# Small operations moved between engines, weight conversions spread over a slot: attention and a bilinear FFN on one Trainium2 core

## The chip, the core and the metric

The kernel runs on one core of a Trainium2 chip. A core has TensorE (PE, matrix products into PSUM), VectorE (DVE), ScalarE (ACT), GpSimd (POOL, which works on SBUF only here) and DMA queues issued mostly by SyncE (SP). Each engine runs its own instructions in the order of the program and waits on semaphores for the others. The metric is device time of one execution in microseconds (us), the median of several runs.

## The reference

An attention block with a threshold feeds a bilinear FFN. Everything is float32 on input and output; the three FFN weights arrive as float64 and are turned into float32 on the chip.

```python
# q, k, v: (8 batches, 8 heads, 576 rows, 64)    tau: 0.02
scores = scale * np.matmul(q, k.transpose(0, 1, 3, 2))
thresh = np.max(scores, axis=-1, keepdims=True) - tau
scores = np.where(scores >= thresh, scores, -1000000000.0)
scores = scores - np.max(scores, axis=-1, keepdims=True)
attn = np.exp(scores)
attn = attn / (np.sum(attn, axis=-1, keepdims=True) + 1e-09)
x = np.matmul(attn, v)          # reshaped to (4608, 512)
# ... w_a, w_b: (512, 1536), w_out: (1536, 512)
out = ((x @ w_a) * (x @ w_b)) @ w_out
```

## The kernel before

The program is a list of 160 units of attention (a pair of heads, a block of rows), one in each slot g, with matmuls of the FFN handed out between them by `advance(cols)`, which issues FFN steps until so many columns are done. The first 16 slots also convert the weights: 36 pieces of 128 x 512 float64 numbers, two or three a slot. A piece takes two activations on ScalarE (upper half and lower half), a clamp on GpSimd, then, one slot later, a sign and a shift on VectorE and an integer add on GpSimd:

```python
    def convert_first(n):
        if n not in raws:
            return
        raw, top = raws[n], pieces[n][0]
        low = work.tile([P, CW], FP32, tag="osb", bufs=OSB_BUFS, name="low")
        nc.scalar.activation(top, raw[:, :, 1].bitcast(FP32), AF.Abs)
        nc.scalar.activation(low, raw[:, :, 0], AF.Copy, bias=2.0, scale=2.0 ** -51)
        stages[n] = low
    def convert_clamp(n):
        if n in stages:
            top = pieces[n][0]
            nc.gpsimd.tensor_scalar(top, top, float_of(0x47EFFFFF), float_of(0x38000000),
                                    op0=ALU.min, op1=ALU.max)
    def convert_sign(n):
        if n in stages:
            low, hi = stages[n].bitcast(U32), raws.pop(n)[:, :, 1]
            nc.vector.scalar_tensor_tensor(out=low, in0=hi, scalar=0x80000000, in1=low,
                                           op0=ALU.bitwise_and, op1=ALU.bitwise_or)
            if n in taken:
                extra.append(taken.pop(n))
    def convert_shift(n):
        if n in stages:
            top = pieces[n][0].bitcast(U32)
            nc.vector.tensor_scalar(top, top, 3, None, op0=ALU.logical_shift_left)
    def convert_add(n):
        if n in stages:
            top, low = pieces[n][0].bitcast(I32), stages.pop(n).bitcast(I32)
            nc.gpsimd.tensor_tensor(top, top, low, op=ALU.add)
            state["converted"] += 1
```

In a slot the scores are made by TensorE, the maxima of their rows by VectorE; a bias for the exponential and a threshold for the mask follow, on GpSimd until the sums of the output weights are made (`state["sums"]`, slot 20), afterwards on ScalarE and VectorE:

```python
        mx = small.tile([P, 2], FP32, tag="mx", name="mx")
        thr = small.tile([P, 2], FP32, tag="thr", name="thr")
        bias = small.tile([P, 2], FP32, tag="bias", name="bias")
        for j in range(n):
            c = slice(j, j + 1)
            nc.vector.tensor_reduce(mx[:, c], sc[j], axis=AX.XY, op=ALU.max)
            if not state["sums"]:
                nc.gpsimd.tensor_scalar(bias[:, c], mx[:, c], e_nscale, None, op0=ALU.mult)
        engine = nc.vector if state["sums"] else nc.gpsimd
        engine.tensor_scalar(thr[:, 0:n], mx[:, 0:n], cut, None, op0=ALU.subtract)
        scored[i, u] = (sc, thr, bias, mx, not state["sums"])

    def weigh(i, u):
        sc, thr, bias, mx, biased = scored.pop((i, u))
        n = len(sc)
        sums = small.tile([P, 2], FP32, tag="sums", name="sums")
        ws = rooms_of(i, u)
        sb = [s.rearrange("p c (n e) -> p c n e", e=Q) for s in sc]
        wb = [w.rearrange("p (c n) e -> p c n e", c=2) for w in ws]
        for j in range(n):
            if not biased:
                nc.scalar.activation(bias[:, j:j + 1], mx[:, j:j + 1], AF.Copy, scale=e_nscale)
            nc.scalar.activation(wb[j], sb[j], AF.Exp, bias=bias[:, j:j + 1], scale=e_scale)
        for j in range(n):
            wv = wb[j]
            nc.vector.scalar_tensor_tensor(
                out=wv, in0=sb[j], scalar=thr[:, j:j + 1], in1=wv,
                op0=ALU.is_ge, op1=ALU.mult, accum_out=sums[:, j:j + 1])
        weights[i, u] = (ws, sums)
```

`sc` holds two of the four PSUM tiles until the mask has read them. In the first eight slots (BY_PE = 8) the normalised weights are turned by TensorE with a diagonal matrix of reciprocals; after that ScalarE normalises and VectorE transposes blocks, with a swap through DRAM:

```python
    def reciprocal(i, u, engine):
        ws, sums = weights[i, u]
        n = len(ws)
        if engine is nc.scalar:
            nc.scalar.activation(sums[:, 0:n], sums[:, 0:n], AF.Copy, bias=1e-9)
        else:
            nc.vector.tensor_scalar_add(sums[:, 0:n], sums[:, 0:n], 1e-9)
        rcp = small.tile([P, 2], FP32, tag="rcp", name="rcp")
        nc.vector.reciprocal(rcp[:, 0:n], sums[:, 0:n])
        weights[i, u] = (ws, rcp)
# ...
    def diagonals(i, u):
        ws, rcp = weights[i, u]
        dg = work.tile([P, 2, P], FP32, tag="h", bufs=H_BUFS, name="dg")
        for j in range(2):
            nc.scalar.activation(dg[:, j], ident, AF.Copy, scale=rcp[:, j:j + 1])
        weights[i, u] = (ws, dg)

    def turn_pe(i, u):
        ws, dg = weights.pop((i, u))
        ws = [w.rearrange("p n e -> p (n e)") for w in ws]
        wT = work.tile([P, NSLOT, P], FP32, tag="wT", bufs=WT_BUFS, name="wT")
        turned[i, u, "pe"] = wT
        tp = banks(512, "tp").rearrange("p j (s q) -> p j s q", s=NT)
        for j, w in enumerate(ws):
            for s in range(NT):
                c = TAIL * j + s * P
                nc.tensor.matmul(tp[:, j, s, :], w[:, c:c + P], dg[:, j], start=True, stop=True)
        for j in range(2):
            nc.scalar.copy(wT[:, 5 * j:5 * j + NT], tp[:, j])
        tp = banks(P, "tp")[:, 0]
        for j, w in enumerate(ws):
            c = MAIN * (1 - j)
            nc.tensor.matmul(tp[TAIL * j:TAIL * (j + 1)], w[:, c:c + TAIL], dg[:, j],
                             start=True, stop=True)
        nc.vector.tensor_copy(wT[:, NT], tp)
# ...
def join(out, lo, hi):
    nc.scalar.copy(out, lo)
    nc.vector.tensor_tensor(out, out, hi, op=ALU.add)
```

`weighted_unit` and `weighted` multiply the turned weights with v into `pv`, join it into `xT`, and GpSimd copies `xT` with its halves of partitions swapped into `xS` (`exchange`). The FFN waits, while the program is being written, for the count of converted pieces; its first product goes through ScalarE, its second through VectorE:

```python
        for f, c0, c1 in steps:
            while (state["converted"] < 2 * HP * (f // n + 1)
                   or kind == "first" and state["rows"] * P < c1):
                yield 0, 0, 0
            # ... pab: 32 matmuls for w_a, then 32 for w_b, on xT and xS
                if w is wa_sb:
                    nc.scalar.copy(ht, pab)
                else:
                    nc.vector.tensor_tensor(ht, ht, pab, op=ALU.mult)
```

The loop over slots, with the parts that play a role here:

```python
    for g in range(len(units) + PV_LAG):
        written = len(pending)
        here = g < len(units)
        converting = bool(early.get(g)) or bool(early.get(g - 1))
        if here:
            i, u = units[g]
            scores(i, u)
        turn_back()
        exchange_blocks()
        pace = (PACE if g > BY_PE else PACE_EARLY) * BLOCK_COLS
        if g > BY_PE:
            pace = min(pace, backlog() / (min([a for a in arrivals if a > g] + [len(units) + PV_LAG + 1]) - g))
        pace += (NSLOT + 1) // 2 * S / (NT + 1) + CATCH_UP * max(backlog() - BLOCK_COLS, 0)
        if 2 <= g < BY_PE + 2:
            weighted_unit(*units[g - 2])
            running["owed"] -= (NSLOT + 1) // 2 * P
        if g < 3:
            prep_copy(*prep_pe(g + 1, "q"))
        for n in early.get(g - 1, []):
            convert_sign(n)
        for n in early.get(g - 1, []):
            convert_shift(n)
        for n in early.get(g - 1, [])[-1:] + early.get(g - 1, [])[:-1]:
            convert_add(n)
        if g == 3:
            for c in range(0, NSUM - 2 * CW + 1, 2 * CW):
                extra.append(sums_u32[:, c:c + 2 * CW].rearrange("p (f w) -> p f w", w=2))
        load_weights(RAWS)
        if g > BY_PE and g <= len(units):
            turn_blocks(*units[g - 1])
        if g > BY_PE:
            advance(PORTIONS[0] * pace)
        if here:
            weigh(i, u)
        if 0 < g <= BY_PE:
            turn_pe(*units[g - 1])
        if g < 3:
            prep_copy(*prep_pe(g + 1, "k"))
        for p in range(HP, NPR):
            for name, d in (("q", 2), ("k", 1)):
                if g == first[p] - d:
                    prep(p, name)
        if g > BY_PE:
            advance(PORTIONS[1] * pace)
            n = g - PV_LAG
            if BY_PE <= n < len(units) and part(*units[n]):
                make_room()
                weighted(*part(*units[n]))
                running["owed"] -= (NSLOT + 1) // 2 * width(*part(*units[n]))
        for n in early.get(g, [])[:1]:
            convert_first(n)
            convert_clamp(n)
        if here:
            reciprocal(i, u, nc.scalar if converting else nc.vector)
        if here and g < BY_PE:
            diagonals(i, u)
        elif here:
            normalise(i, u)
        for n in early.get(g, [])[1:]:
            convert_first(n)
            convert_clamp(n)
        load_weights(RAWS)
        for p in range(HP, NPR):
            for name, d in (("q", 4), ("k", 3)):
                if g == first[p] - d:
                    load(p, name)
        for p in range(1, NPR):
            if g == first[p] - 1:
                load_v(p)
        store(written)
        advance((PORTIONS[2] if g > BY_PE else sum(PORTIONS[:3])) * pace)
        advance(PORTIONS[3] * pace)
```

## Time and profile before

| | before |
|---|---|
| median of 3 runs | 1483.07 us (1481.49 to 1487.32) |
| profiled execution, span | 1478.9 us |
| TensorE busy | 1425.3 us, 25344 matmul instructions |
| VectorE, ScalarE, GpSimd busy | 925.8, 669.7, 360.1 us |
| first 160 us: TensorE, VectorE, ScalarE, GpSimd busy | 119.3, 109.6, 100.8, 101.0 us |
| granted clock of TensorE | 0.991 |

In a timeline each line gives the start, the duration, the engine, the line of the kernel (L367 is line 367), the operation, output and inputs by the program's names, the shapes and a count of instructions; in brackets stands how long the engine had been idle before it and what ended that. In this kernel L332 is the maximum, L334 and L363 the bias on GpSimd and on ScalarE, L336 the threshold, L364 the exponential, L367 the mask, L225 and L226 the conversion's activations, L238 and L246 sign and shift, L232 and L251 clamp and add, L584 and L586 the FFN's copy and product into h, L468 and L469 the two halves of a join, L489 the swapped copy, L325 scores, L479 pv, L406 and L412 the transposes and L408 their copies, L578 the FFN's first products.

### The profile page before, as it was taken

What the parts mean: (1) busy time and instruction counts of PE and PEld (TensorE: products, weight loads), DVE (VectorE), ACT (ScalarE), POOL (GpSimd) and SP (SyncE); (2) the same over time, 40 slices, a digit from 0 to 9 for tenths busy, and PEclk for the clock granted to TensorE, in tenths of its full rate; (3) what the DMA queues carried; (4) which work ended last, traced back from release to release, by engine and by line L of the source; (5) the groups of instructions that cost most, each with busy time, mean ns of one, the idle gap of its engine ahead of it and who ended that gap; (6) DMA issues with size and microseconds to landing.
All of it is one profiled execution on the core that took longest, in us unless ns stands there. A gap on an engine that the chain in (4) does not pass through costs nothing.

```text
span 1478.9 us, 57127 instructions
## 1 busy us (share of the span) xinstructions
PE 1425.3 (96%) x25344; PEld 1201.8 (81%) x25344; DVE 925.8 (63%) x2068; ACT 669.7 (45%) x1213; POOL 360.1 (24%) x563
## 2 busy tenths in 40 slices
PE   5777999999999999999999999999999999999998
PEld 4666587898879898898888788889888888888886
DVE  5767677778767776675645766577756766622212
ACT  4766355555544554553533544355444554411010
POOL 3876522204030312122222213130404040310000
PEclk9999999999999999999999999999999999999999
DMA  9957888789868976786547876588756976530000
GB/s 192 214 154 184 169 168 191 175 178 194 209 139 169 193 174 144 176 184 163 125 118 137 183 164 150 119 188 184 158 138 138 193 174 158 135 90 16 2 17 16
DMA packets 624582, 220.75 MB, mean 149 GB/s; under 512 B 542928, under 2 KB 612048, under 8 KB 624336
## 3 DMA queue, kind: packets, MB, share of 16 engines
q1 hardware_dynamic: 621968, 216.52, 66.8%
q8 instruction: 199, 3.26, 0.9%
q10 hardware_dynamic: 2368, 0.59, 0.2%
q14 instruction: 47, 0.39, 0.1%
HBM read 127.40 MB, written 89.65 MB: 147 GB/s over the span
## 4 chain that ended last, share of the span: by engine, by line
PE 86%; DVE 5%; DMA 3%; ACT 2%; SPq 2%; issue 1%; POOL 1%; ACTq 0%; DVEq 0%; POOLq 0%
PE pab L578 47%; PE po L621 19%; PE sc L325 10%; PE pv L479 10%; PE po L665 1%; DVE tw L433 1%; DVE low L238 1%; DVE mx L332 1%; DMA swap<-tw 1%; DVE tw L367 1%; DMA raw<-in_moe_w_b_dram 1%; SPq L206 1%; SPq L151 0%; SPq L441 0%; DMA sums_u<-in_k_dram 0%
## 5 line engine op out<-in xcount | busy, mean ns | idle before, releaser
L332 DVE TENSOR_REDUCE mx<-sc 128x1 f32<-128x576 f32 x288 | 205.1, 749 | 133.0 <-PE sc L325 122.2
L578 PE MATMUL pab<-xS,wa_sb 64*64 64x256 f32 (+1 forms) x3584 | 271.6, 371 | 0.9 <-POOL xS L489 0.9
L578 PE MATMUL pab<-xS,wb_sb 64*64 64x256 f32 (+1 forms) x3584 | 268.2, 372 | 0.0
L325 PE MATMUL sc<-kT,qT 64*64 64x288 f32 x2304 | 243.4, 413 | 19.2 <-DVE kT L312 8.1
L590 POOL TENSOR_TENSOR h<-h 128x256 f32<-128x256 f32 x168 | 117.4, 733 | 542.1 <-PE po L621 539.0
L578 PE MATMUL pab<-xT,wa_sb 64*64 64x256 f32 (+1 forms) x3200 | 237.6, 371 | 5.3 <-POOL thr L336 2.1
L578 PE MATMUL pab<-xT,wb_sb 64*64 64x256 f32 (+1 forms) x3200 | 235.2, 368 | 5.6 <-DVE h L586 4.1
L621 PE MATMUL po<-wo_sb,h 64*64 64x256 f32 x3264 | 240.1, 376 | 0.0
L386 ACT ACTIVATE tw<-tw,rcp 128x576 f32<-128x576 f32 x244 | 176.1, 768 | 130.1 <-DVE rcp L380 129.9
L364 ACT ACTIVATE tw<-sc,bias,scalars 128x576 f32<-128x576 f32 x260 | 214.7, 832 | 38.3 <-POOL bias L334 25.4
L578 PEld LDWEIGHTS pab<-xS,wa_sb 64*64 64x64 f32 x3584 | 192.4, 133 | 31.3 <-POOL xS L489 5.3
L367 DVE SCALAR_TENSOR_TENSOR tw<-sc,thr,tw 128x576 f32<-128x576 f32 x260 | 203.6, 802 | 20.7 <-ACT tw L364 19.8
L578 PEld LDWEIGHTS pab<-xS,wb_sb 64*64 64x64 f32 x3584 | 193.6, 134 | 25.2 <-issue 0.8
L621 PEld LDWEIGHTS po<-wo_sb,h 64*64 64x64 f32 x3264 | 176.0, 132 | 24.8
L578 PEld LDWEIGHTS pab<-xT,wa_sb 64*64 64x64 f32 x3200 | 170.4, 134 | 30.4 <-DVE kept L469 4.3
L578 PEld LDWEIGHTS pab<-xT,wb_sb 64*64 64x64 f32 x3200 | 169.6, 133 | 27.9 <-DVE h L586 4.5
L479 PE MATMUL pv<-wT,vm 64*64 64x320 f32 (+3 forms) x2592 | 187.2, 381 | 3.1 <-ACT h L584 1.6
L325 PEld LDWEIGHTS sc<-kT,qT 64*64 64x64 f32 x2304 | 143.3, 135 | 52.5 <-issue 14.4
L621 PE MATMUL po<-sums_u,h 64*64 64x256 f32 x2448 | 180.6, 376 | 0.0
L433 DVE STREAM_TRANSPOSE tw<-tw 128x576 f32<-128x576 f32 x240 | 171.6, 753 | 0.2 <-ACT tw L386 0.2
L586 DVE TENSOR_TENSOR h<-h,pab 128x512 f32<-128x512 f32 (+1 forms) x112 | 73.3, 655 | 147.9 <-PE pab L578 140.1
L479 PEld LDWEIGHTS pv<-wT,vm 64*64 64x64 f32 x2592 | 141.6, 135 | 26.3 <-issue 2.8
(85 smaller groups left out, 1236.9 us busy)
## 6 DMA issues: line engine op xcount, KB each, us to landing
swap<-tw SPq DMA_DIRECT2D x240, 288.0 KB, 5.2
wT<-swap SPq DMA_DIRECT2D x28, 1440.0 KB, 7.8
wT<-swap SPq DMA_DIRECT2D x32, 1152.0 KB, 6.3
vm<-in_v_dram SPq DMA_DIRECT2D x32, 288.0 KB, 4.8
qT<-in_q_dram SPq DMA_DIRECT2D x112, 72.0 KB, 3.6
kT<-in_k_dram SPq DMA_DIRECT2D x112, 72.0 KB, 5.1
swap<-wt SPq DMA_DIRECT2D x112, 72.0 KB, 2.7
out_dram<-kept SPq DMA_DIRECT2D x30, 256.0 KB, 4.5
```

Of the source, the lines that this page charges most:

```text
L206: engine.dma_start(dst, part)
L325: nc.tensor.matmul(sc[j if u < NT else 0][to, c], qT[r, q0:q0 + D], kT[r, c * SH:(c + 1) * SH], start=True, stop=True)
L332: nc.vector.tensor_reduce(mx[:, c], sc[j], axis=AX.XY, op=ALU.max)
L364: nc.scalar.activation(wb[j], sb[j], AF.Exp, bias=bias[:, j:j + 1], scale=e_scale)
L367: nc.vector.scalar_tensor_tensor(out=wv, in0=sb[j], scalar=thr[:, j:j + 1], in1=wv, op0=ALU.is_ge, op1=ALU.mult, accum_out=sums[:, j:j + 1])
L386: nc.scalar.activation(w, w, AF.Copy, scale=rcp[:, j:j + 1])
L433: nc.vector.transpose(w, w)
L479: nc.tensor.matmul(pv[j * D:(j + 1) * D, r], vm[rows, k0], wT[rows, k0], start=(s == (NT if j == r else 0)), stop=(s == NT - 1))
L578: nc.tensor.matmul(pab[c * D:(c + 1) * D, r], w[rows, f // n, k, fs + c * D:fs + (c + 1) * D], moving, start=(k == 0), stop=(k == H - 1))
L586: nc.vector.tensor_tensor(ht, ht, pab, op=ALU.mult)
L590: (nc.vector if state["over"] else nc.gpsimd).tensor_tensor(*a, **kw)
L621: nc.tensor.matmul(po[c * D:(c + 1) * D, r, y], ht[rows, t0:t0 + D], other[rows, f], start=(f == 0), stop=(f == NF // 2 - 1))
```

## The change

Five things are changed. The bias is made by ScalarE and the threshold by VectorE in every slot, so GpSimd has no part in the softmax. The three steps that end a piece's conversion (sign, shift, add) are no longer done for all pieces at the start of a slot: the first piece's are done there, the second's after the masks and the normalisation, the third's after the FFN's share. In slots 0 to 8 that share of the FFN is issued ahead of the conversions' first steps of the second and third piece. In slots 0 to 7 the reciprocal is taken right after the masks, its sum on VectorE. And since pieces are now finished in the middle of a slot, the count that the FFN looks at is brought up to date only at the start of the next slot. The aim is that masks and h copies need not stand behind conversions in their engines' queues.

```diff
--- before.py
+++ after.py
@@ -182,7 +182,7 @@
         pieces.append((wo_sb[:, F, :], [w_out[F * P:(F + 1) * P, :].bitcast(U32)]))
     NPIECES = len(pieces)
     raws, stages, extra, taken = {}, {}, [], {}
-    state = {"loaded": 0, "converted": 0, "rows": 0, "sums": False, "through": 0, "over": False}
+    state = {"loaded": 0, "added": 0, "converted": 0, "rows": 0, "sums": False, "through": 0, "over": False}
 
 
     NSUM = NF // 2 * 3 * CH
@@ -249,7 +249,7 @@
         if n in stages:
             top, low = pieces[n][0].bitcast(I32), stages.pop(n).bitcast(I32)
             nc.gpsimd.tensor_tensor(top, top, low, op=ALU.add)
-            state["converted"] += 1
+            state["added"] += 1
 
 
     scalars = const.tile([P, 8], FP32, name="scalars")
@@ -330,11 +330,8 @@
         for j in range(n):
             c = slice(j, j + 1)
             nc.vector.tensor_reduce(mx[:, c], sc[j], axis=AX.XY, op=ALU.max)
-            if not state["sums"]:
-                nc.gpsimd.tensor_scalar(bias[:, c], mx[:, c], e_nscale, None, op0=ALU.mult)
-        engine = nc.vector if state["sums"] else nc.gpsimd
-        engine.tensor_scalar(thr[:, 0:n], mx[:, 0:n], cut, None, op0=ALU.subtract)
-        scored[i, u] = (sc, thr, bias, mx, not state["sums"])
+        nc.vector.tensor_scalar(thr[:, 0:n], mx[:, 0:n], cut, None, op0=ALU.subtract)
+        scored[i, u] = (sc, thr, bias, mx)
 
     def rooms_of(i, u):
 
@@ -352,15 +349,14 @@
 
     def weigh(i, u):
 
-        sc, thr, bias, mx, biased = scored.pop((i, u))
+        sc, thr, bias, mx = scored.pop((i, u))
         n = len(sc)
         sums = small.tile([P, 2], FP32, tag="sums", name="sums")
         ws = rooms_of(i, u)
         sb = [s.rearrange("p c (n e) -> p c n e", e=Q) for s in sc]
         wb = [w.rearrange("p (c n) e -> p c n e", c=2) for w in ws]
         for j in range(n):
-            if not biased:
-                nc.scalar.activation(bias[:, j:j + 1], mx[:, j:j + 1], AF.Copy, scale=e_nscale)
+            nc.scalar.activation(bias[:, j:j + 1], mx[:, j:j + 1], AF.Copy, scale=e_nscale)
             nc.scalar.activation(wb[j], sb[j], AF.Exp, bias=bias[:, j:j + 1], scale=e_scale)
         for j in range(n):
             wv = wb[j]
@@ -748,6 +744,14 @@
     for name in ("q", "k"):
         prep_copy(*prep_pe(0, name))
     early = {}
+
+    def convert_rest(g, k):
+
+        for n in early.get(g - 1, [])[k:k + 1]:
+            convert_sign(n)
+            convert_shift(n)
+            convert_add(n)
+
     n = 0
     for g in range(NPIECES):
         size = min(3 if 4 <= g < 10 else 2, NPIECES - n)
@@ -755,6 +759,7 @@
         n += size
     for g in range(len(units) + PV_LAG):
         written = len(pending)
+        state["converted"] = state["added"]
         here = g < len(units)
         converting = bool(early.get(g)) or bool(early.get(g - 1))
         if here:
@@ -771,12 +776,7 @@
             running["owed"] -= (NSLOT + 1) // 2 * P
         if g < 3:
             prep_copy(*prep_pe(g + 1, "q"))
-        for n in early.get(g - 1, []):
-            convert_sign(n)
-        for n in early.get(g - 1, []):
-            convert_shift(n)
-        for n in early.get(g - 1, [])[-1:] + early.get(g - 1, [])[:-1]:
-            convert_add(n)
+        convert_rest(g, 0)
         if g == 3:
             for c in range(0, NSUM - 2 * CW + 1, 2 * CW):
                 extra.append(sums_u32[:, c:c + 2 * CW].rearrange("p (f w) -> p f w", w=2))
@@ -787,6 +787,8 @@
             advance(PORTIONS[0] * pace)
         if here:
             weigh(i, u)
+        if here and g < BY_PE:
+            reciprocal(i, u, nc.vector)
         if 0 < g <= BY_PE:
             turn_pe(*units[g - 1])
         if g < 3:
@@ -805,12 +807,15 @@
         for n in early.get(g, [])[:1]:
             convert_first(n)
             convert_clamp(n)
-        if here:
-            reciprocal(i, u, nc.scalar if converting else nc.vector)
         if here and g < BY_PE:
             diagonals(i, u)
         elif here:
+            reciprocal(i, u, nc.scalar if converting else nc.vector)
             normalise(i, u)
+        convert_rest(g, 1)
+        if g <= BY_PE:
+            advance(pace)
+        convert_rest(g, 2)
         for n in early.get(g, [])[1:]:
             convert_first(n)
             convert_clamp(n)
@@ -823,8 +828,9 @@
             if g == first[p] - 1:
                 load_v(p)
         store(written)
-        advance((PORTIONS[2] if g > BY_PE else sum(PORTIONS[:3])) * pace)
-        advance(PORTIONS[3] * pace)
+        if g > BY_PE:
+            advance(PORTIONS[2] * pace)
+            advance(PORTIONS[3] * pace)
 
         if not converting and not state["sums"]:
             state["slots"] = state.get("slots", 0) + 1
```

## The prediction, made before the changed kernel had run

> **What bounds the kernel now.** I read the page's busy line and its 40 slices first, to see where TensorE has gaps at all.
>
> ```profile
> PE 1425.3 (96%) x25344; PEld 1201.8 (81%) x25344; DVE 925.8 (63%) x2068; ACT 669.7 (45%) x1213; POOL 360.1 (24%) x563
> ...
> PE   5777999999999999999999999999999999999998
> ```
>
> TensorE is busy 1425.3 of 1478.9 us, so only 53.6 us of gaps exist, and the row of digits puts them at the start. Busy time by stretch says it in numbers (columns: stretch, its length, then busy us and instructions of PE, PEld, DVE, ACT, POOL, then granted clock, DMA share, GB/s):
>
> ```profile
> 0.00:160.00 160.00, 119.32 (x2150) 98.17 (x2154) 109.56 (x242) 100.79 (x189) 101.00 (x144) 0.93 0.81 185
> 160.00:230.00 70.00, 68.76 (x1134) 50.12 (x1127) 48.36 (x110) 31.64 (x56) 20.04 (x26) 1.00 0.86 170
> 230.00:1479.00 1249.00, 1237.23 (x22075) 1053.55 (x22067) 767.83 (x1718) 537.28 (x970) 239.03 (x394) 1.00 0.65 144
> ```
>
> In the first 160 us, the 16 slots that convert weights, TensorE has 40.7 us of gaps and VectorE, ScalarE and GpSimd are each busy over 60%, so none alone is the bound: a loop through all of them is. After that TensorE is 98 to 99% busy. The change leaves every matmul in place (same shapes, same counts), and the order of TensorE's work differs in slots 7 to 25 only, where a few groups of FFN matmuls move by one slot. So everything it can win lies in the first 190 us or so, and the ceiling is some 42 us, 2.8%.
>
> Then the timeline of one converting slot, slot 7 (71.8 to 82.1 us), line by line:
>
> ```profile
> 71.83 1.42 DVE L332 TENSOR_REDUCE mx<-sc 128x1 f32<-128x576 f32 x2 [2.04 <-PE sc L325]
> ...
> 73.47 1.56 ACT L364 ACTIVATE tw<-sc,bias,scalars 128x576 f32<-128x576 f32 x2 [0.23 <-POOL bias L334]
> 73.48 1.94 DVE L238 SCALAR_TENSOR_TENSOR low<-raw,low 128x512 uint32<-128x512 uint32 x3
> ...
> 75.76 1.07 ACT L408 COPY wT<-tp 128x512 f32<-128x512 f32 x2 [0.73 <-PE tp L406]
> ...
> 76.54 0.81 DVE L367 SCALAR_TENSOR_TENSOR tw<-sc,thr,tw 128x576 f32<-128x576 f32 x1
> ...
> 80.86 0.66 ACT L226 ACTIVATE low<-sums_u 128x512 f32<-128x512 uint32 x1
> ```
>
> The reader should see two queues. On VectorE the signs of three pieces start at 73.48 and the mask (L367) only at 76.54, though its first exponential ended near 74.3: signs and shifts stand in front of it for 2.2 us. On ScalarE the conversions run to the end of the slot. What that costs TensorE is in the next lines.
>
> ```profile
> 81.42 0.35 ACT L584 COPY h<-pab 128x256 f32<-128x256 f32 x1
> 81.81 0.42 DVE L586 TENSOR_TENSOR h<-h,pab 128x256 f32<-128x256 f32 x1 [3.28 <-ACT h L584]
> ...
> 81.83 0.70 PE L325 MATMUL sc<-kT,qT 64*64 64x288 f32 x4 [0.98 <-ACT h L584]
> ```
>
> The copy of the FFN's first factor (h, L584) waits in ScalarE's queue behind late conversions; VectorE idles 3.28 us for it and TensorE stops in the middle of the next slot's scores.
>
> **What the skill says.** Three places. (1) PSUM — Partial Sum Buffer, section Engine vs sequencer instructions: the queues of ScalarE, VectorE and GpSimd are "strict FIFO". The trace agrees: the h copy starts the moment the last conversion is through. (2) Perfetto Trace Analysis, section Optimizing Scalar/DVE Operations: GpSimd and VectorE share an SBUF port, and a two-port VectorE operation locks it. The trace fits: a bias on GpSimd takes 0.28 us when the port is quiet, but its mean is 549 ns over the first 160 us, and two took 1.91 us at 115.63 beside signs and shifts. (3) ScalarE: Activation LUTs, section What ACT_TABLE_LOAD costs: an activation costs 186 ns plus 0.833 ns per element, and 93 ns for each pointer operand. For one element and a pointer scale I estimate 0.28 us from that page; the trace has the very operation later in the kernel, 287 ns mean (L363).
>
> **The change part by part.** In 'slot g' below, times are those of before.
>
> *Bias to ScalarE, threshold to VectorE.* GpSimd loses 38 biases (18.5 us) and 21 thresholds (10.9 us). ScalarE gains 38 biases of 0.287 us; bias and exponential alternate, and in the later slots such a set of four runs 193.83 to 195.95, about 2.1 us, against 1.56 us for two exponentials alone: +0.57 us a slot. VectorE gains a threshold of 0.25 us. Where ScalarE has slack this costs nothing; where the slot waits for ScalarE it costs. In slots 4 and 5 the transposed weights (wT, L408) start as soon as the exponentials end (48.35, 55.82), so there the 0.57 us is lost, less the 0.20 us of the sum's activation that moves to VectorE in slots 0 to 7: 0.37 us each. Slots 0 to 3 have two pieces and a chain of transposes: slot 0 loses about 0.4 us, since the second exponential ends later and the sum and reciprocal come ahead of the copy of kT; slot 2 wins about 0.4, its mask starting earlier; slot 3 loses 0.2. Sum of slots 0 to 5: +0.9 us.
>
> *h copies ahead of late conversions.* Slots 5 to 8 are tied by one loop with one PSUM buffer: pv, xT on ScalarE and VectorE, tp, wT, the short tp, FFN matmuls, scores, pv. From xT to xT it takes 63.92 to 72.98, that is 9.06 us, in slot 6, where nothing disturbs it. Slot 7 takes 72.98 to 84.14, 11.16 us: 2.1 more. Slot 8 takes 84.14 to 95.07, 10.93 us; pv waits there for the h copy (1.61 us). With h ahead of two conversions both return to about 9.1 us, but slot 8 then ends on ScalarE's own queue, where the late conversions still end at 93.3 less 0.35 and are followed by xT: I count 1.4 us rather than 1.9. Slots 5 and 6 win nothing: pv follows the scores without a gap worth counting. Sum: -3.5 us.
>
> *Signs and shifts split around the masks.* One piece's sign and shift are some 0.62 + 0.34 = 0.96 us. From slot 9 on the transposes and masks stand behind them and TensorE waits for the mask or for the h product after it: 2.67 us at 100.36, 1.55 us at 111.79, 1.39 us at 119.18, 3.72 us at 147.49, 0.69 us at 155.33. Slot 9 moves h behind the masks, which eats most: -0.45. Slot 10 (three pieces) could start its mask 1.9 us earlier, but the pieces that are put off (2.0 us) stand ahead of the next maximum, so VectorE's own work of 8.05 us becomes the limit against 8.67 us now; with the earlier threshold this is -0.6 to -1.0, I take -1.0. Slot 11: -0.8. Slot 12 is bound by TensorE (7.4 us), 0. Slot 13 waits for ScalarE's sum (rcp at 141.09), which stays where it is, 0. Slot 14: -0.6, slot 15: -0.8. In slots 1 to 8 the earlier mask is worth little, for it is not the mask that ends the loop. Sum: -3.65 us.
>
> *A by-product in slot 20.* The FFN waits for the swapped copy of x on GpSimd, which stands behind two biases and a threshold:
>
> ```profile
> 186.36 0.31 POOL L336 TENSOR_SCALAR thr<-mx,scalars 128x2 f32<-128x2 f32 x1
> ...
> 186.74 3.58 POOL L489 COPY xS<-xT 64x256 f32<-64x256 f32 x8
> ...
> 187.18 3.62 PE L578 MATMUL pab<-xS,wa_sb 64*64 64x256 f32 x30 [0.93 <-POOL xS L489]
> ```
>
> xT is complete at 184.44 (the VectorE join of 0.42 us at 184.02), so without the three small operations GpSimd can begin 2.3 us earlier. TensorE then saves the wait of 0.93 us and most of the slow 3.62 us (the same group on xT took 1.94 us): -2.2 us.
>
> *Delay of the conversion count by a slot.* It only moves FFN groups between slots 7 and 25; no matmul is added. 0.
>
> Together +0.9 - 3.5 - 3.65 - 2.2 = -8.45 us. After slot 25 TensorE is full and its work in the same order, so this arrives whole at the end: 1483.07 - 8.45 = 1474.6 us, say 1474.5.
>
> **Rivals.** (a) *ScalarE becomes the bound of the three-piece slots.* Its work there is 3 x 1.22 (conversions, two activations of some 0.61 each) + 2.1 (biases, exponentials) + 1.07 + 0.69 + 0.25 + 0.5 = 8.3 us, against a loop of 9.06 us. For: slots 4 and 5 are bound by it. Against: 0.8 us of room in slots 6 to 8. If it holds, the gain of the h copies goes and the time is about 1479. (b) *Raw weights arrive late.* Signs of later pieces come later in the slot, so their buffers are free later and loads are issued later, while the DMA share is near 1 up to 80 us. For: only four raw buffers up to slot 3. Against: no wait of ScalarE on a raw load is among the waits of before, and conversions of w_out pieces wait for nothing. It would give 1480 to 1487. (c) *The mask's delay is what holds every converting slot.* Then 1 to 2 us would fall from each of slots 4 to 15, some 15 to 20 us in all, and the time is about 1465. Against: the loop of slot 6 has its mask 2 us late and still closes in 9.06 us, on transposes and scores.
>
> **Range and chances.** The terms are small and each could be off by half: 4 us either way. Rival (c) stretches the lower side and rivals (a) and (b) the upper one; three runs of before already spread from 1481.5 to 1487.3. I put 1474.5, with 1465 to 1482. A gain of over 2% needs 29.7 us out of the 42 us there are: 3%. A loss of over 2% would need late loads in every slot: 2%.
>
> **What would show it.** Right: slot 7's scores no longer stop for h; xT to xT is about 9.1 us in slots 7 and 8; the swapped copy in slot 20 follows the join at once; TensorE's gaps up to 160 us shrink by some 6 us, and the stretch after slot 26 keeps its length. Wrong: ScalarE waiting on raw loads (b); ScalarE back to back through slots 6 to 8 with TensorE waiting for wT or xT (a); a fall of a microsecond or more in nearly every slot (c); or a change of length after 230 us, of which this account has none.

## The result, and the profile after

The changed kernel takes 1470.77 us (median; 1469.24 to 1473.64), the kernel before, run beside it, 1482.61 us. The ratio is 0.9916, with a 95% interval of 0.989 to 0.9943. A second comparison in a later batch gave 1469.30 against 1481.08 us, ratio 0.9921 (0.9907 to 0.9934). So 11.8 us are gained; the prediction had 8.45.

From the page of the changed kernel, the busy line and TensorE's slices:

```profile
PE 1420.3 (97%) x25344; PEld 1210.9 (82%) x25344; DVE 942.8 (64%) x2097; ACT 678.4 (46%) x1243; POOL 334.6 (23%) x504
...
PE   5878999999999999999999999999999999999998
```

GpSimd lost 59 instructions, as intended, and TensorE's slices are fuller only at the start. By stretch (columns as in the prediction):

```profile
0.00:160.00 160.00, 125.29 (x2291) 103.33 (x2295) 130.65 (x282) 112.10 (x221) 89.64 (x101) 0.99 0.87 195
160.00:230.00 70.00, 66.67 (x1169) 49.40 (x1165) 52.07 (x116) 35.83 (x66) 6.38 (x9) 0.98 0.90 183
230.00:1479.00 1249.00, 1228.39 (x21898) 1058.17 (x21890) 760.12 (x1701) 530.44 (x958) 238.60 (x394) 1.00 0.65 141
```

In the first 160 us TensorE's gaps fell from 40.7 to 34.7 us, the 6 us that were expected. But a second number moved too, the granted clock, from 0.93 to 0.99: more about it below. Slot 7, line by line:

```profile
68.69 1.41 DVE L332 TENSOR_REDUCE mx<-sc 128x1 f32<-128x576 f32 x2
...
72.17 0.80 DVE L363 SCALAR_TENSOR_TENSOR tw<-sc,thr,tw 128x576 f32<-128x576 f32 x1
...
75.57 1.20 PE L325 MATMUL sc<-kT,qT 64*64 64x288 f32 x16
...
75.78 0.36 ACT L580 COPY h<-pab 128x256 f32<-128x256 f32 x1
```

The mask starts 3.5 us after the first maximum instead of 4.7, the h copy (L580) comes 7.1 us after it instead of 9.6, and the scores are no longer cut in two: all sixteen stand in one row without a wait.

Where the time was gained is read from the start of each slot's first maximum (us from the span's start, slots counted from 0):

| start of slot | before | after | gained so far |
|---|---|---|---|
| 6 | 62.49 | 60.20 | 2.29 |
| 9 | 92.06 | 86.35 | 5.71 |
| 10 | 105.45 | 96.38 | 9.07 |
| 16 | 158.60 | 147.37 | 11.23 |
| 20 | 184.62 | 173.28 | 11.34 |
| 21 | 192.94 | 179.65 | 13.29 |
| 26 | 229.96 | 217.70 | 12.26 |

By slot 26 all is gained. These are single profiled executions, good to about 1 us up to here: a second execution of the changed kernel had 11.37 at slot 26. Behind slot 26 they differ more. The rest takes 1248.9 us in the kernel before, 1254.2 in this execution and 1248.6 in the second, so that this one keeps only 7.0 us of its 12.26 to the end. It ran at half the TensorE clock twice on the way (3.4 us each, from 225.22 and 368.58 us), the second not at all, so the length there goes with the clock and not with the change.

### The profile page after: what moved, and what is told of

Same layout as the page of the kernel before. It is cut to its first block, busy times and chain, and to the rows that moved or that the text cites. A ratio compares the mean times of both kernels' runs of the same rounds, so it can differ in the third digit from the quotient of the medians.

```text
span 1471.9 us, 57132 instructions
## 1 busy us (share of the span) xinstructions
PE 1420.3 (97%) x25344; PEld 1210.9 (82%) x25344; DVE 942.8 (64%) x2097; ACT 678.4 (46%) x1243; POOL 334.6 (23%) x504
## 3 DMA queue, kind: packets, MB, share of 16 engines
q8 instruction: 199, 3.26, 0.9%
## 4 chain that ended last, share of the span: by engine, by line
PE 86%; DVE 6%; DMA 3%; issue 1%; ACT 1%; SPq 1%; DVEq 0%; ACTq 0%
PE pab L574 47%; PE po L617 19%; PE sc L325 10%; PE pv L475 9%; PE po L661 1%; DVE mx L332 1%; DVE tw L363 1%; DVE tw L429 1%; DMA swap<-tw 1%; SPq L437 1%; DMA sums_u<-in_moe_w_a_dram 1%; DVE low L238 1%; DMA kT<-in_k_dram 0%; DMA wT<-swap 0%; PE tp L402 0%
## 5 line engine op out<-in xcount | busy, mean ns | idle before, releaser
L574 PEld LDWEIGHTS pab<-xS,wa_sb 64*64 64x64 f32 x3584 | 196.6, 134 | 29.7 <-issue 3.0
```

Of the source, the lines that this page charges most:

```text
L574: nc.tensor.matmul(pab[c * D:(c + 1) * D, r], w[rows, f // n, k, fs + c * D:fs + (c + 1) * D], moving, start=(k == 0), stop=(k == H - 1))
```

## The experiments

Three parts of the change are undone or done alone: the *small operations* (bias on ScalarE, threshold on VectorE), the *early h* (FFN share ahead of late conversions) and the *split* (signs, shifts and adds around the masks). T1 is the prediction's account; the others are named in the expectations. Waits in this section are sums between 50 and 150 us. The early reciprocal, the fourth part, was never run by itself: it is absent from the runs of one part alone and present in those with one part undone.

**One part alone.** `only_small` is the kernel before with the two hunks of the small operations:

```
-            if not state["sums"]:
-                nc.gpsimd.tensor_scalar(bias[:, c], mx[:, c], e_nscale, ...)
-        engine = nc.vector if state["sums"] else nc.gpsimd
-        engine.tensor_scalar(thr[:, 0:n], mx[:, 0:n], cut, ...)
+        nc.vector.tensor_scalar(thr[:, 0:n], mx[:, 0:n], cut, ...)
...
+            nc.scalar.activation(bias[:, j:j + 1], mx[:, j:j + 1], AF.Copy, scale=e_nscale)
```

> The kernel before with the bias on ScalarE and the threshold on VectorE throughout, and nothing else of the change. T1 (the sums of the prediction): +0.9 us by slot 6, about 0 in slots 6 to 15, -2.2 us in slot 20, so 1481.3 against 1482.6, a difference of -1.3 us. T2 (the earlier mask is what counts, and with it the PSUM buffer that the short transpose gets): the short transpose still waits for ScalarE's copy of wT in slots 6 to 8, so nothing in slots 5 to 8 and the same total as T1. T3 (TensorE's clock in the first 60 us is what gave the changed kernel 2 to 3 us): if the clock follows the program, this run shows scores of 1.2 us and a granted clock near 1 in slots 2 and 3 only if the small operations are what changes it; if it is chance, it differs from execution to execution without regard to the change.

Measured: 1481.24 us against 1480.94, ratio 0.9997 (0.9985 to 1.001). T1's -1.3 us is just inside the interval, but its terms are not what the trace shows: slot 6 starts 2.69 us earlier, not 0.9 later, and slots 6 to 9 lose 1.5 us again. Some of the 2.69 us is the clock's, as is said below.

`only_h` is the kernel before with the FFN share moved and the conversion count taken at the slot's start. It differs in one thing more: signs, shifts and adds stay at the slot's start, but piece by piece, no longer in the order of before.

```
-        for n in early.get(g - 1, []):
-            convert_sign(n)
-        for n in early.get(g - 1, []):
-            convert_shift(n)
-        for n in early.get(g - 1, [])[-1:] + early.get(g - 1, [])[:-1]:
-            convert_add(n)
+        for kk in range(3):
+            convert_rest(g, kk)
...
+        if g <= BY_PE:
+            advance(pace)
         for n in early.get(g, [])[1:]:
             convert_first(n)
...
-        advance((PORTIONS[2] if g > BY_PE else sum(PORTIONS[:3])) * pace)
-        advance(PORTIONS[3] * pace)
+        if g > BY_PE:
+            advance(PORTIONS[2] * pace)
+            advance(PORTIONS[3] * pace)
```

> The kernel before with only the FFN share of the first slots ahead of the late conversions (and the conversion count taken at the slot's start); signs, shifts and adds stay in one block, the small operations stay on GpSimd. T1: -2.1 us in slot 7 and -1.4 us in slot 8, -3.5 us in all (1479.1), the distance from xT to xT about 9.1 us in slots 7 and 8 and unchanged in slots 5 and 6. T2: the same two gains, since its buffers stay as before in slots 6 and 7; nothing in slots 5 and 6. T3: as for the first run of this batch.

Measured: 1481.19 us, ratio 0.9999 (0.9989 to 1.0009): nothing. But this is the early h together with another order, and `no_split` below shows that this order has a price. Five of the 36 shifts take 1.49 to 1.50 us instead of 0.41, three of them in slots 1 to 3, and two in slots 9 and 10. In slot 9 TensorE waits for the masks behind one of them:

```profile
96.32 1.49 DVE L246 TENSOR_SCALAR wa_sb<-wa_sb 128x512 uint32<-128x512 uint32 x1
...
99.92 1.10 PE L579 MATMUL pab<-xT,wb_sb 64*64 64x128 f32 x32 [4.17 <-DVE tw L368]
```

What the early h is worth alone therefore stays open. In slots 6 to 8, where no shift is stretched, the h stall did go (xT to xT in slot 7: 8.62 us instead of 11.16), but slot 8 stayed at 11.10. Its TensorE lines say what took the place:

```profile
86.50 1.10 PE L579 MATMUL pab<-xT,wa_sb 64*64 64x128 f32 x32 [2.14 <-POOL xS L490]
87.39 1.91 PE L579 MATMUL pab<-xS,wa_sb 64*64 64x128 f32 x32
```

Now TensorE waits 2.14 us for the swapped copy of x on GpSimd, and then runs a group of 32 matmuls in 1.91 us that takes 1.05 elsewhere. Whether the new order delayed GpSimd here too was not tested.

`only_split` is the kernel before with `convert_rest` of the diff in its three places, and nothing else (its conversion count too is taken at the slot's start).

> The kernel before with only the signs, shifts and adds split around the masks and diagonals; the small operations stay on GpSimd and the h copies behind the late conversions. T1: nothing up to slot 8, then -0.45, -1.0, -0.8, -0.6, -0.8 us in slots 9, 10, 11, 14 and 15, together -3.65 us (1479.0). T2: besides these, 0.5 to 1 us in each of slots 5 to 7, because the mask comes earlier and the short transpose takes a buffer that VectorE's maximum or mask has left, not one that waits for ScalarE's copy of wT: -5 to -6 us in all (about 1477). T3: any difference within slots 0 to 4 goes with the granted clock and not with waits.

Measured: 1477.55 us, ratio 0.9967 (0.9953 to 0.9982): -3.4 us by the medians, -4.9 by the ratio. T1's size is about right, slots 9 to 15 winning 3.2 us. T2 falls for this kernel: slots 5 to 8 lose 1.0 us where it expected gains. ScalarE's waits in this kernel:

```profile
ACT tw L365 <- POOL bias L335: 14.0, 11, 2.9
```

(us in all, times, the longest.) In the kernel before the same view has 5.8 us for the bias, and 7.8 us in which ScalarE's sums wait for the masks; here the masks' wait is 0.8. The mask no longer stands behind signs and shifts, but the bias comes later, and with it the exponentials. Its slot 7 on GpSimd and ScalarE shows how:

```profile
71.91 1.27 POOL L251 TENSOR_TENSOR wb_sb<-wb_sb,low 128x512 int32<-128x512 int32 x1 [0.36 <-DVE wb_sb L246]
73.16 0.61 POOL L232 TENSOR_SCALAR wb_sb<-wb_sb 128x512 f32<-128x512 f32 x1
...
74.32 1.23 POOL L335 TENSOR_SCALAR bias<-mx,scalars 128x1 f32<-128x1 f32 x2
...
75.33 1.55 ACT L365 ACTIVATE tw<-sc,bias,scalars 128x576 f32<-128x576 f32 x2 [1.46 <-POOL bias L335]
```

Adds put off to the end of a slot, and the clamps behind them, run into the next one, ahead of its bias. The first maximum of that slot had ended at about 72.8; its bias began at 74.32.

**The PSUM buffer.** The order in which TensorE's buffers are handed out changed with the split: in slots 6 to 8 of the kernel before, the short transpose got the buffer of the first transpose and waited for ScalarE's copy of wT. `same_buf` forces that back:

```
-    psum = pool("psum", 4, space=PSUM)
+    psum = pool("psum", 1, space=PSUM)       # and a list: which of four buffers
...
-        return psum.tile([P, 2, 512], FP32, tag="banks", name=name)[:, :, 0:n]
+        tag = "bank" + next(order)           # as in the changed kernel, but for
+        return psum.tile([P, 2, 512], FP32, tag=tag, name=name)[:, :, 0:n]   # 3 of 678
```

> The changed kernel with one thing put back: in slots 6, 7 and 8 the short transpose gets the PSUM buffer of the first transpose of its slot, as in the kernel before, and so waits for ScalarE's copy of wT; all other buffers and all orders stay. T1: the loop is not bound there, so no change (1470.8). T2: the waits come back: +0.9 us in slot 6, +0.4 in slot 7, about 0 in slot 8, together +1.3 us (1472.1). T3: no change, the first 40 us as in the changed kernel.

Measured: 1472.42 us, ratio 0.9933 (0.9912 to 0.9954). The total alone does not separate it from the changed kernel, but the trace does. TensorE's short transpose in slot 6, in `same_buf`:

```profile
65.06 0.44 PE L408 MATMUL tp<-dg,tw 128*64 128x128 f32 x4 [1.16 <-ACT wT L404]
```

and in the changed kernel:

```profile
64.31 0.44 PE L408 MATMUL tp<-dg,tw 128*64 128x128 f32 x4
```

The distance from xT to xT is 9.17, 9.31 and 9.35 us in slots 6, 7 and 8 against 8.10, 8.88 and 9.07: 1.8 us in all. T2 holds: some of the gain came from a buffer that no line of the diff mentions.

**One part undone.** `small_back` is the changed kernel with the first diff of this section reversed.

> The changed kernel with the biases and thresholds back on GpSimd up to the sums, as before; the split and the early h copies stay. The runs of single parts left 7 to 8 us of the gain to no part. Theory T4: on GpSimd the bias stands behind the clamps and adds that the split and the early h copies push into the start of the next slot (ScalarE waited for it 5.8 us between 50 and 150 us before, 8.4 with only the early h, 14.0 with only the split), so without the move of the small operations the rest gains little: 1477 to 1479 us, ScalarE waiting more than 12 us for the bias. Additive theory (each part is worth what it is alone, and the small operations nothing): 1471, no different from the changed kernel.

Measured: 1474.90 us, ratio 0.997 (0.9958 to 0.9981): 5.6 us of the gain are lost by the medians, 7.3 by the ratios, and ScalarE waits 19.2 us for the bias. T4 holds in its mechanism; the time is 2 us below its range.

`h_late` is the changed kernel with the FFN share behind the late conversions again:

```
-        if g <= BY_PE:
-            advance(pace)
         convert_rest(g, 2)
...
-        if g > BY_PE:
+        if g <= BY_PE:
+            advance(pace)
+        else:
             advance(PORTIONS[2] * pace)
```

> The changed kernel with the FFN share of the first slots back at the end of the slot, behind the late conversions; the split and the small operations on ScalarE and VectorE stay. T4: split and small operations belong together, so most of the gain stays: 1473 to 1475 us; what is lost is the h copy waiting behind conversions in slots 7 and 8 (about 2 to 3 us, TensorE waiting for h). Additive theory: the early h gave nothing alone, so 1471; or, with the split's value alone, 1477.5.

Measured: 1473.89 us, ratio 0.9957 (0.9942 to 0.9973). The time is in T4's range, but "most of the gain stays" is too much: by the ratios 6.4 of 11.7 us stay. TensorE waits three times for the h copy before pv, 5.3 us in all, and slots 6 to 8 take 28.7 us from xT to xT instead of 26.1.

`no_split` puts signs, shifts and adds back at the slot's start.

```
-        convert_rest(g, 0)
+        for kk in range(3):
+            convert_rest(g, kk)
...
-        convert_rest(g, 1)
...
-        convert_rest(g, 2)
```

> The changed kernel with all signs, shifts and adds back in one block at the slot's start; the small operations on ScalarE and VectorE and the early h copies stay. T4: the bias no longer waits, but the masks stand behind the signs and shifts and the wait only changes its name (ScalarE's sum waited for the mask 9.7 us with the small operations alone): 1477 to 1480 us. My prediction's sum (split worth 3.65 us): 1474.4. In the additive theory: 1471 plus 3.4, 1474.

Measured: 1504.16 us, ratio 1.0167 (1.0145 to 1.0188). No theory had expected 24 us more than before. The edit had kept the order piece by piece, as in `only_h`, not the one of before, and the trace of slot 7 shows what that does, on VectorE and GpSimd:

```profile
83.24 0.52 DVE L246 TENSOR_SCALAR wa_sb<-wa_sb 128x512 uint32<-128x512 uint32 x1
...
83.99 1.58 POOL L251 TENSOR_TENSOR wa_sb<-wa_sb,low 128x512 int32<-128x512 int32 x1
...
84.37 1.48 DVE L246 TENSOR_SCALAR wb_sb<-wb_sb 128x512 uint32<-128x512 uint32 x1
```

The shift of the second piece meets the add of the first, and takes 1.48 us instead of 0.41; it ends 0.3 us after the add. So it went with 21 of the 36 shifts. The kernel before issues all shifts before any add, and the last piece's add first: none of its shifts is over 0.52 us.

`no_split_block` repeats the run with that order:

```
-        convert_rest(g, 0)
+        for n in early.get(g - 1, []):
+            convert_sign(n)
+        for n in early.get(g - 1, []):
+            convert_shift(n)
+        for n in early.get(g - 1, [])[-1:] + early.get(g - 1, [])[:-1]:
+            convert_add(n)
```

> The changed kernel with signs, shifts and adds in one block at the slot's start in the order of before: all signs, all shifts, then the adds with the last piece's first. The earlier run without the split kept the order piece by piece and took 1504 us; 21 of its 24 slots' shifts took 1.48 to 1.51 us instead of 0.41, each beside the add of the piece before on GpSimd. T5 (the port): with the order of before no shift is over 0.6 us and the 24 us of loss are gone. What is left tells what the split is worth beside the small operations and the early h: T4 says the masks behind the block cost most of the gain, 1476 to 1479 us; the prediction's sum says 1474.4; if the split is worth nothing, 1471.

Measured: 1483.76 us, ratio 1.0018 (1.001 to 1.0027). T5 holds: no shift is over 0.52 us, and 20 us of the loss went with the order that stretched them. But all three numbers for what remains were too low: without the split the rest of the change, the early reciprocal included, is worth less than nothing. (The expectation miscounts: it is 21 shifts of 36.) The loss arises in slots 1 to 4 (5.7 us against before), and this is slot 2:

```profile
38.45 1.27 POOL L251 TENSOR_TENSOR wa_sb<-wa_sb,low 128x512 int32<-128x512 int32 x1
...
38.58 1.17 DVE L374 TENSOR_SCALAR sums<-sums 128x2 f32<-128x2 f32 x1
...
40.05 0.75 DVE L312 COPY kT<-tp 128x576 f32<-128x576 f32 x1
...
40.85 1.81 PE L325 MATMUL sc<-kT,qT 64*64 64x288 f32 x16 [2.65 <-DVE kT L312]
```

The changed kernel adds 1e-9 to the sums (L374) on VectorE, and earlier. Beside an add on GpSimd these two elements take 1.11 to 1.19 us in seven of eight slots; in the changed kernel, where the split has the late adds out of the way, 0.17 in seven of eight. The copy of kT and the next scores stand behind it. So it seems that this small move pays only together with the split, but it was not run by itself.

**What else bounds it.** In slot 19 of the changed kernel VectorE waits for a load of k, and TensorE in slot 20 behind it:

```profile
171.05 0.78 DVE L297 STREAM_TRANSPOSE kT<-kT 128x576 f32<-128x576 f32 x1 [4.54 <-DMA kT<-in_k_dram]
...
171.93 1.32 PE L325 MATMUL sc<-kT,qT 64*64 64x288 f32 x16 [1.40 <-issue]
```

`k_early` issues that load a slot earlier:

```
-                if g == first[p] - d:
+                if g == first[p] - (4 if p == HP else d):
                     load(p, name)
```

> The changed kernel with the load of k for the fifth pair issued one slot earlier, behind that of q in slot 16, and nothing else. In the changed kernel VectorE waits 4.54 us for this load in slot 19 and TensorE 1.40 us before the scores of slot 20, while the kernel before waited 0.55 us and TensorE not at all. If that wait takes back part of the gain, this kernel is faster by the 1.4 us of TensorE's gap, at 1469.4; a rival says that the swapped copy of x or the queue of SyncE takes its place in slot 20 and nothing changes (1470.8).

Measured: 1472.49 us, ratio 0.9946 (0.9927 to 0.9965): no gain, the rival's case. The wait is gone and slot 19 is shorter, 8.12 us instead of 9.58, but slot 20 is longer by 1.8 us and a wait that was not there before stands in slot 21:

```profile
183.14 0.74 PE L475 MATMUL pv<-wT,vm 64*64 64x64 f32 x34 [1.45 <-issue]
```

`after_again` is the changed kernel unaltered, for the comparison within its batch.

> The changed kernel once more, unaltered, beside the other three of this batch and on their chip, so that they are compared with it and not with runs of another chip. All theories: a ratio to before of about 0.992, some 1470 us; the forced order of slots (2 us more from the first transposes' slots by the small operations, 7 us between slots 5 and 10) is seen again in its trace.

Measured: 1469.30 us, ratio 0.9921, as stated above.

`grouped` takes the stretched shifts out of the changed kernel (it has five of 1.50 us):

```
-        for n in early.get(g - 1, [])[k:k + 1]:
+        for n in ns[k:k + 1]:
             convert_sign(n)
             convert_shift(n)
-            convert_add(n)
+        for n in (ns[:1], [], ns[:0:-1])[k]:     # ns: the pieces of the slot before
+            convert_add(n)
```

> The changed kernel, split as it is, but the adds of the second and third piece both behind the third piece's shift, the third's add first, so that no shift runs beside an add. In the changed kernel five shifts (58.05, 67.26, 84.92, 94.61, 104.11 us) took 1.50 us instead of 0.41, 5.4 us of VectorE ahead of the next maximum. T5: no shift over 0.6 us, and 2 to 4 us less in all, about 1467 to 1469. Rival: TensorE has FFN work at those moments and waits for the mask and xT elsewhere, so nothing is gained, 1471; or the later adds hold the FFN's product back and 1 us is lost.

Measured: 1472.03 us, ratio 0.9938 (0.9923 to 0.9953). No shift is over 0.84 us, and nothing is gained: T5's size falls. A stretched shift costs VectorE 1.1 us, but at 84.92 us of the changed kernel, for one, TensorE is busy all through it. In `grouped` the same slot 8 took 10.93 us instead of 8.48, with a gap of TensorE of 2.04 us before the FFN and slow matmuls behind it (see the clock, below); how much of this the later adds caused stays open.

`best` also issues the threshold just ahead of the masks, in `weigh` instead of `scores`.

> The same as the run with grouped adds, and the threshold issued just ahead of the masks instead of just behind the maxima, so that the join of xT on VectorE no longer stands behind it (0.58 us beside GpSimd's clamps; TensorE waited 4.2 us in all for that join between 0 and 150 us). If the join is on the path: another 1 us less, 1466 to 1468. If ScalarE's half of the join is what comes last: the same as with grouped adds alone.

Measured: 1472.56 us, ratio 0.9936 (0.9923 to 0.9949): the same as with grouped adds alone. None of these versions beats the changed kernel.

## Why the prediction was right in its total, and where its steps failed

**The sum.** The total lay in the range, 3.4 us short. Slot by slot, in the profile, the terms came out as -2.29 us for slots 0 to 5 (put at +0.9), -3.42 for 6 to 8 (-3.5), -5.52 for 9 to 15 (-3.65), -2.06 for 16 to 20 (-2.2) and +1.03 for 21 to 25 (0). The first and the third are the ones that were mis-sized. In both stretches the kernel before ran at half clock where the changed kernel did not, and the step that failed is that the working has no term for TensorE's clock (see below); how much of each difference is the clock's stays open. "Together +0.9 - 3.5 - 3.65 - 2.2" fails in another way if its terms are read as values of the parts, as T1 did:

| kernel | ratio | interval | ScalarE waits for GpSimd's bias | ScalarE waits for the masks' sums | TensorE waits for ScalarE's h before scores and pv |
|---|---|---|---|---|---|
| before | 1 | | 5.8 | 7.8 | 2.6 |
| small operations alone | 0.9997 | 0.9985–1.001 | 0 | 9.7 | 4.1 |
| early h, in another order | 0.9999 | 0.9989–1.0009 | 8.4 | 10.1 | 0 |
| split alone | 0.9967 | 0.9953–0.9982 | 14.0 | 0.8 | 4.0 |
| without the small operations | 0.997 | 0.9958–0.9981 | 19.2 | 0.8 | 0 |
| without the early h | 0.9957 | 0.9942–0.9973 | 0 | 5.3 | 5.3 |
| without the split | 1.0018 | 1.001–1.0027 | 0 | 8.5 | 0 |
| whole change | 0.9921 | 0.9907–0.9934 | 0 | 5.7 | 0 |

Alone, the small operations are worth 0.4 us and the split 4.9 (1481.08 times the shortfall of each ratio); all together give 11.7. The clearest comparison is among the four kernels that have the split. On top of it the small operations bring 1.5 us and the early h -0.4, but both together 6.8 (the early reciprocal counted with each; every one of these differences is good to some 3 us). Their waits show why. With the split alone two queues remain, GpSimd's in front of the bias (14.0 us) and ScalarE's in front of h (4.0). Either part ends one of these waits and leaves the other longer, 5.3 or 19.2 us; only both end both. What the split does for the masks is less clear. Their wait falls to 0.8 us only where the exponentials themselves come late, and is 5.7 in the changed kernel against 7.8 before. Nor do these sums rank the kernels: without the split they add up to 8.5 us against 16.2 before, and that kernel is the slower.

**Bias and threshold.** "+0.9" for slots 0 to 5 became a gain, 2.29 us in the changed kernel and 2.69 in `only_small` (0.58 and 0.70 of it ahead of the first maximum), but this does not refute its working. TensorE ran at half clock four times before slot 6 in the profile of before (3.4 us each, from 19.47, 26.30, 36.54 and 57.02 us), three times in `only_small` and once in the changed kernel. Slots 0 to 5 of `only_small` gained -0.88, 1.12, 0.70, -0.21, -0.57 and 1.84 us. The two large gains are in slots 1 and 5, where the kernel before lost clock; in slots 2, 3 and 4 the prediction had gains of 0.4, -0.2 and -0.37. What the move is worth without the clock stays open. In slot 5 of the kernel before, one line invites another reading:

```profile
55.03 1.54 POOL L336 TENSOR_SCALAR thr<-mx,scalars 128x2 f32<-128x2 f32 x1
...
55.82 1.06 ACT L408 COPY wT<-tp 128x512 f32<-128x512 f32 x2
...
56.98 1.99 PE L578 MATMUL pab<-xT,wa_sb 64*64 64x128 f32 x32 [2.12 <-POOL thr L336]
```

It puts TensorE's wait of 2.12 us down to the threshold. But the threshold had ended at 56.57. The trace's record of semaphores has TensorE's queue waiting for ScalarE until 56.93, and ScalarE's copy of wT ended at 56.88. So the chain is the one that the prediction had for this slot, wT behind the exponentials, and not the threshold.

**Early h.** -3.5 us for slots 6 to 8 is what those slots gained (5.71 less 2.29 is 3.42 us). Its division is off: slots 6, 7, 8 gained 0.85, 1.13 and 1.44, not 0, 2.1 and 1.4. The claim that "nothing disturbs" the loop of slot 6 at 9.06 us was wrong: it contained a wait of 1.22 us for ScalarE's wT, through a PSUM buffer, and closes in 8.10. This is not yet rival (c): `same_buf` has the masks as early as the changed kernel and needs 9.17 us there. Taken out of the whole, the early h is worth about 5 us (0.9957 less 0.9921); what it is worth alone stays open.

**Split.** -3.65 us for slots 9 to 15 became 5.52 (11.23 less 5.71), and of this 3.36 fell in slot 9, for which I had put 0.45. The kernel before shows there:

```profile
100.36 1.10 PE L578 MATMUL pab<-xT,wb_sb 64*64 64x128 f32 x32 [2.67 <-DVE h L586]
101.28 1.84 PE L578 MATMUL pab<-xS,wb_sb 64*64 64x128 f32 x32
...
103.73 1.71 PE L325 MATMUL sc<-kT,qT 64*64 64x288 f32 x16
```

I counted the gap of 2.67 us. I did not count what followed it: a group in 1.84 us that takes 1.05 otherwise, and scores in 1.71 that take 1.20. Between 101.39 and 104.80 us the granted clock is 0.50.

**Slot 20.** -2.2 us was right for the swapped copy (slot 20 itself gained 1.95), but slot 19 gave 2.54 back to the load of k, which the prediction had not looked at. That slots 16 to 18 gained 2.65 us, which it had not foreseen either, and so made the sum come out, is luck. `k_early` did not get the loss back.

**The clock, the term that was missing.** The Trainium skill, TensorE: Matmul & The Clock Gate, Part 1: The HAM clock gate, says that TensorE falls to half its clock after idling for a window of some 3.4 us, that the window runs freely, and that the same kernel therefore differs from run to run. The traces agree with the window and with what follows from it: the granted clock is always 1.0 or 0.5, each stretch at half clock within the program is 3.41 us long or twice that, and all of one profile lie on one grid of 3.41 us, which lies differently in the next profile. They differ in the condition: the window before need not be idle. Twice the same wait, in `k_early`:

```profile
81.54 1.88 PE L574 MATMUL pab<-xT,wa_sb 64*64 64x128 f32 x32 [1.73 <-DVE tw L363]
```

and in `after_again`:

```profile
82.68 1.10 PE L574 MATMUL pab<-xT,wa_sb 64*64 64x128 f32 x32 [1.73 <-DVE tw L363]
```

With the two groups of 32 that follow, the first takes 5.11 us and the second 3.26. The windows of the grid say why, the one with the wait and the next (columns as in the prediction). In `k_early`:

```profile
78.30:81.71 3.41, 1.38 (x17) 0.97 (x20) 3.38 (x8) 3.38 (x7) 3.20 (x6) 1.00 0.48 150
81.71:85.12 3.41, 3.41 (x71) 3.41 (x70) 3.35 (x8) 2.10 (x4) 2.45 (x3) 0.50 0.57 195
```

and in `after_again`:

```profile
80.43:83.84 3.41, 1.60 (x47) 1.39 (x51) 3.34 (x10) 3.18 (x7) 3.20 (x5) 1.00 0.57 174
83.84:87.25 3.41, 3.41 (x114) 3.37 (x109) 3.41 (x5) 3.41 (x7) 2.08 (x3) 1.00 0.59 207
```

In the first, TensorE was busy 1.38 us of the window, 40%, and the next window was at half clock. In the second it was busy 1.60 us, 47%, and the next was not. Counted over the fourteen profiled executions of this study, from 18 to 277 us, a window at full clock was followed by one at half clock in 28 of 28 cases where TensorE had been busy less than 40% of it, in 19 of 29 from 40 to 50%, in 4 of 47 from 50 to 60% and in 2 of 883 above. So it matters how much of one window a gap takes. Where the grid lies is chance: the two profiles of the changed kernel have a clock of 0.94 and 0.89 between 30 and 60 us, which is T3's second answer.

The kernel still moves the average. In the first 160 us there are 7 windows at half clock in the kernel before, 5, 4 and 4 in `only_small`, `only_h` and `only_split`, 5 without the small operations, 6 without the split in block order, and 1 and 3 in the profiles of the changed kernel. The granted clock of the first 160 us averages 0.948 over those six kernels and 0.974 over the seven other profiles, `no_split` left out; 0.026 of 160 us is 4 us. Over all executions of the last batch the clock averaged 0.9933 for the kernel before (27) and 0.9958 for the changed kernel (6); 0.0025 of the span is 3.7 us. Both are estimates and upper bounds, since TensorE does not have work all that time, but they have the size of the 3.4 us that the prediction fell short. That the clock is the reason for that whole difference was argued from these counts, not tested by a run of its own.

**Rivals (a) and (b).** ScalarE does run without a pause in slot 7 from 73.05 us on, and xT begins at 78.34, behind the last conversion, though pv had ended at 77.86. But the loop still closes in 8.88 us: (a) did not decide. (b) is seen as waits of 1.0 and 0.3 us on raw loads about slot 5, and no more.

## What to carry to other kernels

When several queues stand in front of the same step, a change to one is worth little until the others are shortened as well: test parts both alone and taken out of the whole, and do not add their values. Before moving work to a later place in one engine's queue, ask which engine's queue it then enters, here GpSimd's, and what of the next slot stands behind it. And count for a gap of TensorE more than its length where it leaves TensorE busy less than about half of some 3.4 us, as the counts above show for this kernel.

## What the runs showed of the hardware

- A VectorE shift of 128x512 (one source, 0.41 us) beside a GpSimd add of the same size takes 1.48 to 1.52 us and ends 0.3 us after the add; a VectorE operation on 128x2 takes 1.11 to 1.19 us instead of 0.17. Masks (0.81 us) and maxima (0.75 us each) did not lengthen: beside such adds the changed kernel has 16 masks of at most 0.82 and 24 maxima of at most 0.77 us.
- The order of issue decides whether they meet: piece by piece 1504.16 us, all shifts ahead of the adds 1483.76.
- TensorE's granted clock is 1.0 or 0.5 for whole windows of 3.41 us. The half came after each of the 28 full-clock windows in which TensorE was busy less than 40%, and after 2 of 883 in which it was busy over 60%. Two such windows in a row, in `after_again` from 53.13 us, made three groups of 32 matmuls take 1.99, 1.96 and 1.96 us instead of about 1.1.
- Which PSUM buffer a pool hands out can change with the order of other instructions, and cost 1.16 us at one transpose.
